# Sums of activations: their stores and loads move from SyncE's DMA queue to GpSimd's

## The chip, the cores and the metric

One core of a Trainium2 chip runs the whole program. The metric is device time in microseconds (us) of one execution; the kernel before takes 1059.25 us (median of three runs, 1059.17 to 1061.05). A core has TensorE (PE) for matmuls, VectorE (DVE), ScalarE (ACT), GpSimd (POOL) and SyncE (SP), which run side by side and wait for each other by semaphores. SP and POOL both issue DMAs here, each in the order of its own program: an instruction that waits holds up all that stand behind it on the same engine.

## The reference

```
x   = attention(q, k, v, w_phi)            # linear attention, 4 x 8 heads, 576 tokens, 64 wide
x   = (sigmoid(x @ w_gate) * (x @ w_val)) @ w_out     # 2304 tokens, 512 -> 1536 -> 512
out = leaky(x @ w_in2) @ w_out2            # 512 -> 2048 -> 512, leaky(h) = max(0.01 h, h)
```

The weights of both layers come as 64-bit floats and are decoded on the chip.

## The kernel before

**Precision.** Each operand of a matmul is kept as a high and a low part in fp32r, and a product is three matmuls (lines 52 to 54). A `gh`/`gl` pair is the two parts of a hidden activation: ACT makes `gh` (line 48), DVE makes `gl` (line 49), PE reads both.

**Stages.** Attention runs first, about 286 us, with the first units of the gated layer mixed in. Then the gated layer goes through its 1536 hidden columns in chunks of 256 (`c` = 0 to 5), and the second layer through its 2048 in eight. The tokens are five blocks: four of 512 (`b` = 0 to 3) and one of 256. Chunks 0 and 1 of the gated layer multiply block by block (`up_plain`). From chunk 2 on two blocks and two column halves are taken together by seven products instead of eight (`quad`), which needs sums and differences of the blocks of activations.

**The activation sums.** `first_sums` (line 756) makes them for one pair of blocks during chunk 1: it loads four tiles `acc` of 128x1024 from DRAM (`xd`, line 761), forms four sums on DVE (`sum_steps`, line 739), splits each into a high part on ACT (line 749) and a low part on DVE (line 750), and stores both to DRAM (`td`, line 754). Pair 0 comes first; pair 1 starts when pair 0 is done. Later, `swap` reloads them from `td` by GpSimd (line 785), or for the second layer makes them anew with `sum_parts`, stores included.

**The weights.** `decoded` (line 145) is a stream: raw 64-bit halves of 512 KB are fetched by SP into three rotating buffers (`fetch`, line 122), and six DVE and two ACT steps (lines 102 to 114) turn one into a high and a low part. A fetch waits until DVE has read the buffer that it fills. `ahead(n)` advances the stream between matmuls; `need(key)` runs it until a given piece is there; `hold` names the first piece that it may not start.

**Partial sums.** The second product of a chunk (`down1_piece`, line 666) goes from PSUM (`ps_p`, three banks) through an ACT copy (line 678) into one of six staging halves, and GpSimd adds it to DRAM with an accumulating DMA (`accd`, line 679). The next matmul group in that bank waits for the ACT copy.

**Order.** The program is written in one sequence, and a scheduling layer fixes the order of the instructions on each engine when it is built. DVE and ACT execute strictly in that order.

Of the kernel before, what the change touches and what calls it, by code (L numbers as in the profile page):

```python
# [9 lines left out]
F32 = mybir.dt.float32  # L10
# [9 lines left out]
def linear_attention_moe(ctx, tc, q, k, v, w_phi, w_gate, w_val, w_out, w_in2, w_out2, out):  # L20
    nc = tc.nc
# [43 lines left out]
    xd = [dr.tile([128, KD, MAIN], F32, name=f"xd{b}") for b in range(B)]  # L65
# [7 lines left out]
    def take(dt, name="w"):  # L73
        pool, tag = free.popleft()
        return pool.tile([128, 1024], dt, tag=tag, name=name), (pool, tag)

    def give(*slots):
        free.extend(place for _, place in slots)
# [112 lines left out]
    def drop(*key):  # L191
        r = wts.pop(key)
        give(*(r[k] for k in ("hi", "lo", "sh", "sl") if k in r))


    def hidden(h, key, src):
        w = src.shape[1]
        hi = pools["hp"].tile([128, 512], F32R, tag="gh", name="gh")[:, :w]
        lo = pools["hp"].tile([128, 512], F32R, tag="gl", name="gl")[:, :w]
        split(src, hi, lo)  # L200
        h[key] = (hi, lo)
# [274 lines left out]
    def new_pair(b, c):  # L476
        p = Pair()
        p.b, p.c = b, c
        p.kf, p.tq, p.qf, p.u = [], [], [], []
        return p  # L480
# [7 lines left out]
    n = o = oo = None  # L488
# [38 lines left out]
    for i in range(NP + 1):  # L527
        oo, o, n = o, n, (new_pair(*pairs[i]) if i < NP else None)
# [87 lines left out]
    hold = [(3, 0)]  # L616
# [11 lines left out]
    def need(*key):  # L628
        while key not in wts:
            if next(stream, None) is not True and key not in wts:  # L630
                raise RuntimeError(f"no room for {key}: {len(free)} slots free")
# [4 lines left out]
    def gap(n):  # L636
        for _ in range(n):
            if pend:
                pend.popleft()()
# [15 lines left out]
    def load_acc(b):  # L655

        for i in range(1 if b == B else 2):
            acc(1, b, 2 * i)
            a = sums[1, b, i][0]
            if b == B:  # L660
                nc.sync.dma_start(out=a.rearrange("p (k t) -> p k t", k=KD), in_=accd[b])
            else:
                nc.sync.dma_start(out=a.rearrange("p (k t) -> p k t", k=2), in_=accd[b][:, 2 * i:2 * i + 2])
# [25 lines left out]
    def up_plain(l, c, b, steps):  # L689
        w = bw[b]  # L690
        h = {}
        for f in range(CH):
            fs = slice(128 * f, 128 * f + 128)
            ps = []
            for i in range(2 if l == 1 else 1):
                need(l, c, i)
                wt = wts[l, c, i]
                p = bank("u", w)
                for kk in range(KD):
                    mm3(p, wt["vhi"][:, kk, fs], wt["vlo"][:, kk, fs], xpart(xh, b, kk), xpart(xl, b, kk), kk == 0, kk == KD - 1)  # L700
                ps.append(p)
                if l == 1 and i == 0:
                    th = tile2(w)
                    nc.scalar.activation(out=th, in_=p, func=ACTF.Tanh, scale=0.5)
            if l == 1:
                nc.vector.scalar_tensor_tensor(out=th, in0=th, scalar=1.0, in1=ps[1], op0=ALU.add, op1=ALU.mult)
                hidden(h, (f, b), th)
                if f == 0:
                    gap(4)
            else:  # L710
                leaky(h, (f, b), ps[0], True)
            ahead(steps)
        return h
# [17 lines left out]
    td = {}  # L731
    ts = {}

    def sum_steps(l, pair):

        f = {(j, i): sums[l - 1, 2 * pair + i, j][0] for j in range(2) for i in range(2)}
        b11, b12, b21, b22 = (f[j, i] for j in range(2) for i in range(2))
        for o, x, y in ((b11, b12, b11), (b12, b22, b12), (b22, b22, b11), (b21, b21, b22)):
            nc.vector.tensor_tensor(out=o, in0=x, in1=y, op=ALU.subtract)
            yield True  # L740
# [3 lines left out]
    def sum_parts(l, pair, n, s):  # L744

        j, i = PLACE[n]
        src = sums.pop((l - 1, 2 * pair + i, j))
        hi, lo = s[0][0], s[1][0]
        nc.scalar.copy(hi, src[0])
        nc.vector.tensor_tensor(out=lo, in0=src[0], in1=hi.bitcast(F32), op=ALU.subtract)  # L750
        give(src)
        td[l, pair, n] = dr.tile([128, 2, 1024], F32, name=f"td{l}{pair}{n}", tag=f"td{l}{pair}{n}")
        for k in range(2):
            nc.sync.dma_start(out=td[l, pair, n][:, k], in_=s[k][0].bitcast(F32))

    def first_sums(pair, stay):

        for i in range(2):
            for j in range(2):
                s = sums[0, 2 * pair + i, j] = take(F32, "acc")  # L760
                nc.sync.dma_start(out=s[0].rearrange("p (k t) -> p k t", k=2), in_=xd[2 * pair + i][:, 2 * j:2 * j + 2])
        for _ in range(14):
            yield True
        yield from sum_steps(1, pair)
        held = deque()
        for n in (2, 1, 3, 4):
            if len(held) == 2:
                give(*held.popleft())
            s = [take(F32R) for _ in range(2)]
            sum_parts(1, pair, n, s)  # L770
            if stay:
                ts[n] = s
            else:
                held.append(s)
            yield True
            yield True
        if not stay:
            for _ in range(4):
                yield True
        for s in held:  # L780
            give(*s)
# [9 lines left out]
    def swap(l, pair, n):  # L791

        ts[n] = [retake(s) for s in ts[n]]
        if (l, pair, n) in td:
            load_sums(l, pair, n)
        else:
            sum_parts(l, pair, n, ts[n])
# [66 lines left out]
    def up_pair1(c, pair, between, then):  # L864
        h, th = {}, {}
        for i, t in quad(1, c, 0, pair, (1, 1, 1, 1, 1, 0), lambda n: None):
            th[i] = halves[6 + i]
            nc.scalar.activation(out=th[i], in_=t, func=ACTF.Tanh, scale=0.5)
        between()
        for i, t in quad(1, c, 1, pair, (1, 1, 1, 0, 0, 0), then):  # L870
            nc.vector.scalar_tensor_tensor(out=th[i], in0=th[i], scalar=1.0, in1=t, op0=ALU.add, op1=ALU.mult)
            hidden(h, (i // 2, 2 * pair + i % 2), th[i])
        return h
# [38 lines left out]
    for b in range(B - 1, NB):  # L912
        h = up_plain(1, 0, b, 14)
# [6 lines left out]
    for b in range(NB):  # L920
# [6 lines left out]
        h = up_plain(1, 1, b, 5)  # L927
# [16 lines left out]
    for c in range(2, NC1):  # L944
        final = c == NC1 - 1
        if final:
            units = [0, 1, B]
        for n, u in enumerate(units):
            if u == B:
                h = up_plain(1, c, B, 2)  # L950
            elif not final:
                h = up_pair1(c, u, (lambda: drop(1, c, 0)) if n == 2 else (lambda: None),
                             (lambda k, u=u: swap(1, 1 - u, k)) if n == 0 else keep)
            elif u == 0:
                def between():
                    need(1, c, 1)
                    need(1, c, 2)
                    hold[0] = 2, 0

                def then(k):  # L960
                    swap(1, 1, k)
                    if k == 4:
                        gap(2)
                        load_acc(0)
                        load_acc(1)
                h = up_pair1(c, 0, between, then)
            else:
                def between():
                    gap(100)
                    drop_sums(1, c, 0)  # L970
                    side.append(sum_steps(2, 0))

                def then(k):
                    for g in side:
                        for _ in g:
                            pass
                    side.clear()
                    swap(2, 0, k)
                give(*fixed[:3])
                hold[0] = 2, 1  # L980
                h = up_pair1(c, 1, between, then)
                drop_sums(1, c, 1)
                for b in (2, 3, B):
                    load_acc(b)
                reserve[0] = 0
            gap(100)
            if n == 2:
                if final:
                    drop(1, c, 0)
                drop(1, c, 1)  # L990
            queue1(c, u, h)
            if n == 2:
                pend.append(lambda c=c: drop(1, c, 2))
        units = units[::-1]
# [7 lines left out]
    for c in range(NC2):  # L1002
        for n, u in enumerate(units):
            if u == B:
                h = up_plain(2, c, B, 1)
                gap(3)
            else:
                h = up_pair2(c, u, (lambda k, u=u: swap(2, 1 - u, k)) if n == 0 else keep)
# [41 lines left out]
```

## Time and profile before

| | |
|---|---|
| median of three runs | 1059.25 us (1059.17 to 1061.05) |
| the profiled execution | 1059.2 us; its span from first to last instruction 1057.4 us; mean granted clock 0.995 |
| PE busy | 1022.5 us, 97% of the span |
| DVE, ACT, POOL busy | 779.9, 519.6, 169.6 us |
| raw weight loads by SP | 68 of 512 KB, median 4.4 to 5.8 us from issue to landing by tensor |
| `td` stores by SP | 32 of 512 KB, median 5.0 us |
| `xd` loads by SP | 8 of 512 KB, median 8.2 us |
| `td` reloads by POOL | 88 of 512 KB, median 6.2 us |

A row of the timeline gives the start in us from the span's start, the length, engine, line, operation and what is written from what; in brackets, how long the engine stood idle before it and what ended that. A row of the windows gives for each engine the busy time and in parentheses the number of instructions, then the granted TensorE clock (1.00 is 2.4 GHz), the busy share of the DMA engines and GB/s.

### The profile page before, as it was taken

How to read it: one execution, taken by the hardware profiler on the slowest of the kernel's cores; microseconds unless marked ns; L12 is line 12 of the kernel's file. 1: busy time of each engine (PE TensorE's matmuls, PEld its weight loads, DVE VectorE, ACT ScalarE, POOL GpSimd, SP SyncE). 2: the span in 40 equal slices, each digit the busy share in tenths (PEclk: the TensorE clock that was granted, in tenths of full speed). 3: DMA queues.
4: the chain of work that ended last, by engine and by line, in shares of the span. 5: the costliest groups of instructions: out<-in, count | busy, mean ns of one | idle time of the engine just before them, and what ended most of it. 6: DMA issues, size and time to landing. Idle time of an engine off the chain costs nothing.

```text
span 1057.4 us, 15006 instructions
## 1 busy us (share of the span) xinstructions
PE 1022.5 (97%) x5410; PEld 870.3 (82%) x5410; DVE 779.9 (74%) x1373; ACT 519.6 (49%) x1066; POOL 169.6 (16%) x217
## 2 busy tenths in 40 slices
PE   7999999999999989999999989899999999999998
PEld 6788989889788778888888868788888888888886
DVE  4964877766489748395784859998797887979555
ACT  4666676767456535354454434477343333434221
POOL 0122121212201123323233120001010010101000
PEclk9999999999999999999999999999999999999999
DMA  5633343332287978769499493546161542415143
GB/s 142 162 97 93 85 111 99 82 104 75 75 304 224 349 130 256 99 153 260 66 251 187 93 303 147 209 145 221 58 233 63 183 143 97 176 63 179 42 164 134
DMA packets 119481, 160.06 MB, mean 151 GB/s; under 512 B 68720, under 2 KB 71408, under 8 KB 119408
## 3 DMA queue, kind: packets, MB, share of 16 engines
q1 hardware_dynamic: 95216, 94.09, 28.4%
q0 software_dynamic: 24192, 65.02, 24.4%
q8 instruction: 43, 0.70, 0.3%
q14 instruction: 30, 0.25, 0.1%
HBM read 109.64 MB, written 49.36 MB: 150 GB/s over the span
## 4 chain that ended last, share of the span: by engine, by line
PE 76%; issue 6%; DVE 6%; DMA 4%; ACT 3%; POOL 2%; SPq 2%; POOLq 0%; DVEq 0%; ACTq 0%
PE ps_u L53 11%; PE ps_u L52 11%; PE ps_u L54 11%; PE ps_p L52 11%; PE ps_p L54 10%; PE ps_p L53 10%; PE kv L395 4%; PE ps_n L445 2%; POOL accd L679 1%; DMA raw<-in_moe_w_gate_dram 1%; DVE ql L430 1%; POOL rb L467 1%; PE ps_q L413 1%; DMA rb<-rd 1%; DMA w<-td 1%
## 5 line engine op out<-in xcount | busy, mean ns | idle before, releaser
L824 DVE TENSOR_TENSOR q<-ps_u,q 128x512 f32<-128x512 f32 x160 | 109.8, 687 | 63.9 <-PE ps_u L54 57.7
L53 PE MATMUL ps_u<-xl,w 128*128 128x512 f32 (+1 forms) x432 | 152.0, 352 | 0.6 <-DVE xl L686 0.6
L54 PE MATMUL ps_u<-xh,w 128*128 128x512 f32 (+1 forms) x432 | 151.3, 351 | 0.0
L52 PE MATMUL ps_u<-xh,w 128*128 128x512 f32 (+1 forms) x432 | 151.3, 351 | 0.0
L894 DVE TENSOR_TENSOR acc<-acc,ps_p 128x512 f32<-128x512 f32 x126 | 86.2, 684 | 39.5 <-PE ps_p L54 39.0
L52 PE MATMUL ps_p<-w,gh 128*128 128x512 f32 x288 | 112.2, 390 | 0.0
L53 PE MATMUL ps_p<-w,gh 128*128 128x512 f32 x288 | 112.0, 389 | 0.0
L54 PE MATMUL ps_p<-w,gl 128*128 128x512 f32 x288 | 111.7, 389 | 0.0
L785 POOL DMA_DIRECT2D w<-td x88 | 48.6, 559 | 381.9 <-PE ps_u L54 366.5
L679 POOL DMA_DIRECT2D accd<-w x80 | 70.9, 891 | 229.7 <-ACT w L678 159.3
L52 PE MATMUL ps_u<-w 128*128 128x512 f32 x256 | 100.5, 393 | 1.1 <-DVE q L824 1.0
L53 PE MATMUL ps_u<-w 128*128 128x512 f32 x256 | 100.4, 392 | 0.0
L54 PE MATMUL ps_u<-w 128*128 128x512 f32 x256 | 99.9, 391 | 0.0
L53 PEld LDWEIGHTS ps_u<-xl,w 128*128 128x128 f32 x432 | 82.3, 190 | 11.8 <-DVE xl L686 0.8
L52 PEld LDWEIGHTS ps_u<-xh,w 128*128 128x128 f32 x432 | 82.0, 190 | 11.4
L54 PEld LDWEIGHTS ps_u<-xh,w 128*128 128x128 f32 x432 | 82.3, 190 | 10.8
L52 PE MATMUL ps_p<-gh,w 128*128 128x512 f32 (+1 forms) x216 | 79.0, 372 | 8.5 <-ACT gh L48 4.8
L467 POOL TENSOR_TENSOR rb<-u,rb 64x576 f32<-64x576 f32 x32 | 48.7, 1521 | 234.4 <-DMA rb<-rd 116.6
L717 ACT ACTIVATE q<-q 128x512 f32<-128x512 f32 x48 | 30.2, 632 | 112.1 <-DVE q L824 112.0
L53 PE MATMUL ps_p<-gl,w 128*128 128x512 f32 (+1 forms) x216 | 79.9, 371 | 4.1 <-DVE gl L49 3.9
L54 PE MATMUL ps_p<-gh,w 128*128 128x512 f32 (+1 forms) x216 | 79.7, 370 | 0.0
L49 DVE TENSOR_TENSOR gl<-q,gh 128x512 fp32r<-128x512 f32 (+1 forms) x102 | 61.8, 614 | 19.8 <-ACT gh L48 19.6
(151 smaller groups left out, 2304.0 us busy)
## 6 DMA issues: line engine op xcount, KB each, us to landing
w<-td POOLq DMA_DIRECT2D x88, 512.0 KB, 6.2
td<-w SPq DMA_DIRECT2D x32, 512.0 KB, 5.0
accd<-w POOLq DMA_DIRECT2D x64, 256.0 KB, 6.1
raw<-in_moe_w_out_dram SPq DMA_DIRECT2D x28, 512.0 KB, 4.5
raw<-in_moe_w_in_dram SPq DMA_DIRECT2D x16, 512.0 KB, 4.4
raw<-in_moe_w_gate_dram SPq DMA_DIRECT2D x12, 512.0 KB, 5.8
raw<-in_moe_w_val_dram SPq DMA_DIRECT2D x12, 512.0 KB, 5.0
rb<-rd SPq DMA_DIRECT2D x32, 144.0 KB, 3.1
```

Source lines behind the costliest of these rows:

```text
L49: nc.vector.tensor_tensor(out=lo, in0=src, in1=hi.bitcast(F32), op=ALU.subtract)
L52: nc.tensor.matmul(ps, lh, rh, start=first, stop=False, **kw)
L53: nc.tensor.matmul(ps, lh, rl, start=False, stop=False, **kw)
L54: nc.tensor.matmul(ps, ll, rh, start=False, stop=last, **kw)
L395: nc.tensor.matmul(ps[:, h], p.kf[j // 2][:, j % 2, h, s, :], vf[:, j, 64 * h:64 * h + 65], start=(h, j) == (0, 0), stop=False)
L445: nc.tensor.matmul(ps2, w[0], x[0], start=s == 0, stop=s == 1)
L467: nc.gpsimd.tensor_tensor(out=p.rb[sl], in0=p.u[h][sl], in1=p.rb[sl], op=ALU.mult)
L679: nc.gpsimd.dma_start(out=accd[b][:, e], in_=st, accum_op=ALU.add)
L717: nc.scalar.activation(out=th, in_=t, func=ACTF.Lrelu)
L785: nc.gpsimd.dma_start(out=ts[n][k][0].bitcast(F32), in_=td[l, pair, n][:, k])
L824: nc.vector.tensor_tensor(out=o, in0=x, in1=y, op=ALU.add)
L894: nc.vector.tensor_tensor(out=a, in0=a, in1=po, op=ALU.add)
```

## The change

The `td` stores of `sum_parts` and the `xd` loads of `first_sums` are issued by GpSimd instead of SP: 32 stores and 8 loads of 512 KB. In the last chunk of the gated layer the two `need` calls between the two products of the first pair go, and `hold` is set before the first product instead.

```diff
--- before.py
+++ after.py
@@ -751,14 +751,14 @@
         give(src)
         td[l, pair, n] = dr.tile([128, 2, 1024], F32, name=f"td{l}{pair}{n}", tag=f"td{l}{pair}{n}")
         for k in range(2):
-            nc.sync.dma_start(out=td[l, pair, n][:, k], in_=s[k][0].bitcast(F32))
+            nc.gpsimd.dma_start(out=td[l, pair, n][:, k], in_=s[k][0].bitcast(F32))
 
     def first_sums(pair, stay):
 
         for i in range(2):
             for j in range(2):
                 s = sums[0, 2 * pair + i, j] = take(F32, "acc")
-                nc.sync.dma_start(out=s[0].rearrange("p (k t) -> p k t", k=2), in_=xd[2 * pair + i][:, 2 * j:2 * j + 2])
+                nc.gpsimd.dma_start(out=s[0].rearrange("p (k t) -> p k t", k=2), in_=xd[2 * pair + i][:, 2 * j:2 * j + 2])
         for _ in range(14):
             yield True
         yield from sum_steps(1, pair)
@@ -952,10 +952,7 @@
                 h = up_pair1(c, u, (lambda: drop(1, c, 0)) if n == 2 else (lambda: None),
                              (lambda k, u=u: swap(1, 1 - u, k)) if n == 0 else keep)
             elif u == 0:
-                def between():
-                    need(1, c, 1)
-                    need(1, c, 2)
-                    hold[0] = 2, 0
+                hold[0] = 2, 0
 
                 def then(k):
                     swap(1, 1, k)
@@ -963,7 +960,7 @@
                         gap(2)
                         load_acc(0)
                         load_acc(1)
-                h = up_pair1(c, 0, between, then)
+                h = up_pair1(c, 0, lambda: None, then)
             else:
                 def between():
                     gap(100)
```

The places where order changes: the start of chunk 0's last blocks, on SP. `raw` is a fetch of weights, `accd` a partial sum, `acc<-xd` a load for the sums, `td` a store of a sum. Before:

```order
L122 DMA raw<-in_moe_w_gate_dram 128x2x512
L229 DMA accd_3624<-st 128x512
L122 DMA raw<-in_moe_w_gate_dram 128x2x512
L122 DMA raw<-in_moe_w_val_dram 128x2x512 x2
L761 DMA acc<-xd_96 128x1024 x2
L122 DMA raw<-in_moe_w_out_dram 128x1024
L761 DMA acc<-xd_97 128x1024 x2
L122 DMA raw<-in_moe_w_out_dram 128x1024
```

The four loads stood behind four fetches; they are gone from this queue. The same stretch and the next on POOL, now (`rb` is the attention's last product):

```order
L467 TENSOR_TENSOR rb<-u_3524,rb 64x576
L761 DMA acc<-xd_96 128x1024 x2
L761 DMA acc<-xd_97 128x1024 x2
L754 DMA td_4164<-w 128x1024
L754 DMA td_4171<-w 128x1024
L754 DMA td_4157<-w 128x1024
L679 DMA accd_1871<-w 128x512 x2
L754 DMA td_4157<-w 128x1024
L679 DMA accd_1871<-w 128x512
L754 DMA td_4164<-w 128x1024
L679 DMA accd_1871<-w 128x512
L754 DMA td_4171<-w 128x1024
```

They now stand first after the attention's last product, with nothing ahead of them, and the stores of pair 0 stand between the accumulating DMAs. Before, POOL had only the accumulating DMAs (L679) here. On DVE, where the sums of pair 1 begin, before:

```order
L102 TENSOR_SCALAR e_4633<-raw_4071 128x512
L111 SCALAR_TENSOR_TENSOR m_4502<-m_4502,e_4543 128x512
L109 SCALAR_TENSOR_TENSOR e_4633<-raw_4071,e_4633 128x512
L706 SCALAR_TENSOR_TENSOR q_4227<-q_4227,ps_u_4229 128x512
L49 TENSOR_TENSOR gl_4244<-q_4227,gh_4243 128x512
L739 TENSOR_TENSOR acc_4254<-acc_4258,acc_4254 128x1024
```

and now:

```order
L102 TENSOR_SCALAR e_4633<-raw_4071 128x512
L111 SCALAR_TENSOR_TENSOR m_4502<-m_4502,e_4543 128x512
L102 TENSOR_SCALAR e_4679<-raw_4541 128x512
L109 SCALAR_TENSOR_TENSOR e_4633<-raw_4071,e_4633 128x512
L706 SCALAR_TENSOR_TENSOR q_4227<-q_4227,ps_u_4229 128x512
L109 SCALAR_TENSOR_TENSOR e_4679<-raw_4541,e_4679 128x512
L49 TENSOR_TENSOR gl_4244<-q_4227,gh_4243 128x512
L739 TENSOR_TENSOR acc_4254<-acc_4258,acc_4254 128x1024
```

Two steps of decoding the next raw half (L102 and L109 of `e_4679`) moved ahead of the first sum (L739); they stood behind the fourth L750 before. Some 25 rows later a hidden activation (L706 of `q_4431`) now follows L102 of `e_4793` at once and stood behind L109 of it before. On PE the rows are the same; on DVE and ACT nothing else moved, in the last chunk of the gated layer nothing at all.

## Rows read from the trace of the kernel before

**Rows 1.** The page's first part: busy us, share, instructions.

```profile
PE 1022.5 (97%) x5410; PEld 870.3 (82%) x5410; DVE 779.9 (74%) x1373; ACT 519.6 (49%) x1066; POOL 169.6 (16%) x217
```

**Rows 2.** Waits of PE, 286 to 540 us: total us, times, longest.

```profile
PE ps_p L52 <- ACT gh L48: 4.8, 2, 3.4
PE ps_p L52 <- ACT w L678: 1.3, 1, 1.3
PE ps_p L53 <- DVE gl L49: 0.2, 1, 0.2
```

**Rows 3.** Windows behind the two longer of these waits.

```profile
304.00:308.00 4.00, 4.00 (x23) 3.34 (x22) 4.00 (x9) 2.94 (x6) 0.00 (x0) 1.00 0.92 312
...
380.00:384.00 4.00, 1.78 (x5) 1.23 (x6) 2.74 (x5) 1.59 (x4) 0.00 (x0) 0.88 0.03 8
384.00:388.00 4.00, 4.00 (x14) 3.18 (x13) 0.00 (x0) 1.01 (x3) 1.61 (x2) 0.69 0.49 59
```

**Rows 4.** Timeline of DVE from the end of attention.

```profile
294.46 0.43 DVE L102 TENSOR_SCALAR e<-raw 128x512 int32<-128x512 int32 x1 [6.95 <-issue]
...
297.72 0.43 DVE L102 TENSOR_SCALAR e<-raw 128x512 int32<-128x512 int32 x1
...
301.75 0.68 DVE L706 SCALAR_TENSOR_TENSOR q<-q,ps_u 128x512 f32<-128x512 f32 x1
```

**Rows 5.** Timeline of SP's DMA issues, same stretch.

```profile
289.26 0.39 SPq L122 DMA_DIRECT2D raw<-in_moe_w_gate_dram  x1
...
297.00 0.94 SPq L761 DMA_DIRECT2D acc<-xd  x2
```

**Rows 6.** Timeline of POOL: first issue after attention; four reloads in a burst.

```profile
332.13 1.96 POOL L679 DMA_DIRECT2D accd<-w  x2 [46.13 <-DVE acc L739]
...
408.99 2.52 POOL L785 DMA_DIRECT2D w<-td  x4 [0.30 <-PE ps_u L54]
```

**Rows 7.** Two gate fetches by line: issue, then us to landing.

```profile
L122 SPq DMA_DIRECT2D raw<-in_moe_w_gate_dram x1: 427/427/427, 291.2 to 291.2; - x1
...
DMA to landing us min/median/max: 6.5/6.5/6.5
...
L122 SPq DMA_DIRECT2D raw<-in_moe_w_gate_dram x1: 379/379/379, 409.3 to 409.3; - x1
...
DMA to landing us min/median/max: 9.6/9.6/9.6
```

**Rows 8.** Windows: accumulating DMAs start; the sums of pair 1 are loaded.

```profile
332.00:338.00 6.00, 6.00 (x28) 4.95 (x28) 6.00 (x9) 3.86 (x6) 3.61 (x4) 1.00 0.83 177
...
335.00:354.00 19.00, 19.00 (x85) 15.76 (x84) 13.78 (x23) 7.48 (x13) 3.03 (x4) 1.00 1.04 324
```

**Rows 9.** Timeline of SP: loads for pair 1, then two fetches.

```profile
340.40 5.24 SPq L761 DMA_DIRECT2D acc<-xd  x4
345.74 0.41 SPq L122 DMA_DIRECT2D raw<-in_moe_w_out_dram  x1
346.25 0.38 SPq L122 DMA_DIRECT2D raw<-in_moe_w_gate_dram  x1
```

**Rows 10.** Timeline of DVE around the sums of pair 1.

```profile
341.09 0.69 DVE L109 SCALAR_TENSOR_TENSOR e<-raw,e 128x512 int32<-128x512 int32 x1
...
352.52 2.50 DVE L739 TENSOR_TENSOR acc<-acc 128x1024 f32<-128x1024 f32 x2 [4.20 <-DMA acc<-xd]
...
366.06 0.68 DVE L706 SCALAR_TENSOR_TENSOR q<-q,ps_u 128x512 f32<-128x512 f32 x1
...
370.87 1.28 DVE L107 SCALAR_TENSOR_TENSOR m<-raw,m 128x512 f32<-128x512 uint32 x2
...
378.79 0.43 DVE L102 TENSOR_SCALAR e<-raw 128x512 int32<-128x512 int32 x1 [3.60 <-DMA raw<-in_moe_w_gate_dram]
...
380.62 0.68 DVE L706 SCALAR_TENSOR_TENSOR q<-q,ps_u 128x512 f32<-128x512 f32 x1
```

**Rows 11.** The chain that ended last, 365 to 385 us: start, us, what.

```profile
371.58 7.11 DMA raw<-in_moe_w_gate_dram
```

**Rows 12.** Waits of PE, 540 to 720 us.

```profile
PE ps_p L53 <- DVE gl L49: 3.7, 1, 3.7
```

## Prediction

> **What bounds the kernel now.** I read the busy shares first, then PE's waits by stretch, then DVE's timeline at each wait, then the DMA issues that DVE waits for. PE is busy for 97% of the span [rows 1], so the time can change by little more than PE's idle time and its time at a lower clock. The change touches DMAs between 297 and 365 us (chunk 1, where the sums are made) and between 652 and 695 us (the sums for the second layer). From 286 to 540 us PE waits four times, 6.3 us in all: 1.4 us near 303, 1.3 us near 367, and 3.4 + 0.2 us at 382 [rows 2]. The granted clock stays at 1.00 behind the wait of 1.4 us and falls to 0.88 and 0.69 in the two windows around and behind that of 3.4 us [rows 3], which is the lower level (1.2 GHz) for part of them: 4 x 0.12 + 4 x 0.31 = 1.7 us lost. The 382 us wait thus costs 5.3 us.
>
> All of them end at DVE or at ACT work that DVE feeds, and DVE is late because of transfers. At the end of attention it stands idle for 6.95 us until the first raw half is there (294.46), takes the second at 297.72, and comes in its order to the hidden activation L706 at 301.75 [rows 4], from which ACT makes the `gh` that PE waits for. At 352.52 it has waited 4.20 us for the loads of pair 1's sums [rows 10]. At 378.79 it has waited 3.60 us for a gate fetch [rows 10] that was issued at 371.58 and took 7.11 us [rows 11]; L706 at 380.62 stands behind that.
>
> **The change part by part.** The profiled execution took 1059.2 us, its span is 1057.4 us, and the median is 1059.25 us; I add to 1059.2.
>
> *The first loads of sums go earlier.* On SP they are issued from 297.00, behind four fetches [rows 5]. On POOL they stand first, and POOL issues nothing until 332.13 [rows 6]. They need what the first fetch needs, the end of attention in that memory, so they go when it goes, 289.26 [rows 5], 7.7 us earlier, four in a burst of some 2.5 us like the reloads of 408.99 [rows 6]. Nobody wants them that early: the first sum stands far behind on DVE. But the fetches at 289 and 291, for which DVE is idle, now share the DMA engines with 2 MB of sums. The second took 6.5 us without such a burst; the gate fetch at 409.3, beside the burst of reloads, took 9.6 us [rows 7]. By these the second raw half is 0 to 3.1 us later. From 294.46 on DVE is a chain without slack, in which 297.72 to 301.75 is step on step, and PE already waits at its end, so the delay goes to DVE and PE alike. The row of 409.3 is the nearest, but there up to eight loads were queued, here four: I take +2.3 us. The wait of 1.4 us becomes 3.7 us in one or two pieces; if in one, the lower clock follows as at 382 us, up to 1.7 us for PE alone. That extra lag is mostly taken back in the waits at 367 and 382 us, where PE waits for DVE anyway; what of it passes to DVE, since L706 needs PE's product, I put at +0.3 us (0 to 1.7).
>
> On how two issuing engines share, the rows above show a fetch 3.1 us slower beside POOL's burst. The Trainium skill, "DMA: Bandwidth & Descriptors" (Queues, rings and completion order; Issuing engines are not separate DMA queues), says that all queues run on the same 16 DMA engines, which take packets from them in turn, so another issuer brings no bandwidth. The row agrees; by the opposite view, separate paths, this term would be 0.
>
> *The loads for pair 1.* On SP they go out at 340.40 to 345.64, and two fetches wait behind them until 345.74 and 346.25 [rows 9]. From 335 to 354 us the DMA engines are full (share 1.04, 324 GB/s) [rows 8], so order decides and not issue. On POOL the loads cannot go earlier (they stand behind the last store of pair 0), and stores, accumulations and loads keep their order among themselves. What changes is SP: the first fetch can go when DVE has read its buffer, at 341.09 + 0.69 = 341.8 [rows 10], the second some 3 us later, and both take their share ahead of the loads. Two times 0.52 MB at 324 GB/s are 3.2 us. The sums start between 0 and 3.2 us later; I take +2.2.
>
> *DVE's order behind it.* From the first sum to the end of the first L107 are 370.87 + 0.6 - 352.52 = 19 us [rows 10], of which L102 and L109 of the moved half, 0.4 + 0.6 us, now fall into the wait ahead of the sums: -1.0. The gate fetch that follows meets no stores of SP's any more: 7.1 us [rows 11] to 6.5 us [rows 7], -0.4 (0 to -0.6). L706 then follows L102 at once, not L109 after an ACT step: 380.62 - 378.79 = 1.83 us become 0.4 to 0.5 [rows 10]: -1.3. With the sums' +2.2 the wait at 382 us ends 0.5 us earlier, set against the shift of 2.3 + 0.3. PE comes to it later by up to 1.7 us if its clock fell at 303, so the wait itself shrinks from 3.4 to about 2 us, between the 1.4 that kept the clock and the 3.4 that did not [rows 2, 3]: half a chance to save 1.7, -0.8.
>
> *Stores between accumulations.* A waiting store holds up the accumulating DMAs behind it on POOL, these the staging halves, these ACT's copy and PE's banks. The first four are issued from 332.13, and the halves are wanted again from 354 on: nothing, up to 2 us if stores land late. POOL's issues take 3.61 / 4 = 0.9 us each while DVE is busy for 6.00 of 6 us [rows 8], and 2.52 / 4 = 0.6 us in the burst [rows 6]; twelve in 11 us fit.
>
> *652 to 695 us, and the `need` calls.* The order on PE, DVE and ACT stays there, and the longest wait of PE, 3.7 us [rows 12], lies ahead of the first store. Nothing. The last-chunk edit alone moves nothing: the pieces that it no longer forces are asked for by the product that follows.
>
> Sum: +2.3 + 0.3 - 0.5 - 0.8 = +1.3; 1059.2 + 1.3 = **1060.5 us**.
>
> **Rivals.**
> 1. *The fetches keep their pace, faster.* DMA bandwidth at 289 to 297 us suffices, +0; the pair-1 fetches slip in without holding up the sums, +0. Then 1.0 + 0.4 + 1.3 = 2.7 us off at 382 us, the wait near 367 goes with an L706 two instructions earlier, and with the lower clock gone 1.7 more: 1059.2 - 2.7 to -4.4, about 1055.4. For it: the fetch at 291 still landed in 6.5 us with three others in flight. Against it: the row of 409.3.
> 2. *The full price, slower.* Decided at 289 us: if the second raw half lands over 3 us later, +3.1; the lower clock behind the longer wait passes to DVE whole, +1.7; the sums come 3.2 late, which leaves 3.2 - 1.0 - 1.3 = +0.9, and the clock still falls at 382. 1059.2 + 5.7 = 1064.9. For it: DVE has no slack from 294 to 348 us. Against it: four loads, not eight.
> 3. *POOL cannot issue beside DVE.* Longer issues would delay sums and accumulations together. The four issues of 0.9 us at a DVE that never paused [rows 8] speak against it; with the 0.3 us between 0.9 and 0.6, twelve issues cost 3.6 us, 1062.8, if all lay on the path. The Trainium skill, "SBUF — State Buffer" (SBUF: two separate sides, the trap "DVE blocks DMA"; A bandwidth-pool intuition that's wrong), says that GpSimd cannot write descriptors while DVE holds their shared port, and gives 620 ns against 3100 ns: by it twelve issues would cost 30 us, an estimate, about 1089. The row does not show it.
> 4. *The change does nothing that counts*: both collisions stay small, 1059.2.
>
> **How the numbers follow.** Less than 0.2% (2.1 us) cannot be told from no change here. My forecast, with rival 4 beside it, spans 1058 to 1062.5 and gets 0.44: 0.36 of it within 0.2%, 0.02 faster, 0.06 slower. Rival 1: 0.25, of it 0.23 faster. Rival 2: 0.27, of it 0.24 slower. Rival 3: 0.04, of it 0.03 slower. Together faster 0.25, same 0.42, slower 0.33. The range 1055.5 to 1064.5 reaches to the middle of rivals 1 and 2.
>
> **What would show it.** The four loads of `acc` on POOL near 289 to 292 us; DVE's L102 of 297.72 later by about 2.3 us and PE's wait near 303 of about 3.7 us; the first sum of pair 1 some 2 us later still; PE's wait at 382 us shorter, with the clock at 1.00 or nearly. From 400 us on PE's waits as before. I am wrong if the second raw half lands within 7 us of its issue, if the sums of pair 1 start earlier than before relative to PE, or if PE's waits after 540 us change.

## The result and the profile after

The changed kernel takes 1066.07 us (median of seven runs, 1064.81 to 1070.02); seven runs of the kernel before beside them have a median of 1061.05 us. The ratio is 1.0053, with a 95% interval of 1.0033 to 1.0073: slower by 5.6 us (the medians lie 5.0 us apart). The profiled execution took 1064.81 us, its span is 1063.0 us, 5.6 us longer than before. The prediction had 1060.5 us and a range up to 1064.5. It added to 1059.2 us, and seven runs put the kernel before 1.8 us higher, which is not the change's doing; 5.6 us added to 1059.2 are 1064.8, also outside the range.

PE's busy time grew by 1.9 us [rows 1] and its idle time by 3.7. The page's first part, changed kernel:

```profile
PE 1024.4 (96%) x5410; PEld 871.6 (82%) x5410; DVE 780.3 (73%) x1373; ACT 519.9 (49%) x1066; POOL 191.8 (18%) x257
```

PE's waits from 286 to 540 us, changed kernel (total us, times, longest): 10.7 us against 6.3 [rows 2].

```profile
PE ps_p L52 <- ACT gh L48: 5.7, 2, 3.3
PE ps_p L52 <- ACT w L678: 2.2, 1, 2.2
PE ps_p L53 <- DVE gl L49: 2.1, 2, 1.7
PE ps_u L52 <- ACT q L704: 0.7, 1, 0.7
```

Where they lie, in the timeline of PE (start, length; in brackets the wait and what ended it):

```profile
298.45 0.39 PE L52 MATMUL ps_u<-xh,w 128*128 128x256 f32 x1 [0.71 <-ACT q L704]
302.12 0.50 PE L53 MATMUL ps_p<-gl,w 128*128 128x512 f32 x1 [1.75 <-DVE gl L49]
306.45 0.73 PE L52 MATMUL ps_p<-gh,w 128*128 128x512 f32 x2 [2.42 <-ACT gh L48]
...
356.95 0.50 PE L52 MATMUL ps_p<-gh,w 128*128 128x512 f32 x1 [2.19 <-ACT w L678]
...
387.21 0.50 PE L52 MATMUL ps_p<-gh,w 128*128 128x512 f32 x1 [3.26 <-ACT gh L48]
```

Three waits stand where one of 1.4 us stood. Windows behind the third of them and behind the last; the third number from the end is the granted clock, and they answer to [rows 3]:

```profile
304.00:308.00 4.00, 1.58 (x7) 1.32 (x7) 4.00 (x9) 1.82 (x3) 0.00 (x0) 0.92 0.34 131
308.00:312.00 4.00, 4.00 (x14) 3.21 (x13) 3.69 (x8) 2.69 (x5) 0.00 (x0) 0.66 0.33 89
...
388.00:392.00 4.00, 3.97 (x12) 3.19 (x13) 0.73 (x2) 1.58 (x3) 1.05 (x2) 0.66 0.24 21
```

From 304 to 312 us the clock is at its lower level (1.2 GHz) for part of the time: 4 x 0.08 + 4 x 0.34 = 1.7 us, which were not lost there before. The cause stands in the DMA issues at the end of attention, which answer to [rows 5] and [rows 6]. POOL's, in its timeline:

```profile
289.22 2.29 POOL L761 DMA_DIRECT2D acc<-xd  x4 [3.90 <-issue]
```

and SP's, in the same stretch:

```profile
288.58 0.39 SPq L122 DMA_DIRECT2D raw<-in_moe_w_gate_dram  x1
290.18 0.32 SPq L229 DMA_DIRECT2D accd<-st  x1
290.55 0.43 SPq L122 DMA_DIRECT2D raw<-in_moe_w_gate_dram  x1
```

The timeline of DVE shows who waits for them; it answers to [rows 4] and [rows 10]:

```profile
298.43 0.69 DVE L706 SCALAR_TENSOR_TENSOR q<-q,ps_u 128x512 f32<-128x512 f32 x1 [3.43 <-ACT q L704]
...
301.04 0.43 DVE L102 TENSOR_SCALAR e<-raw 128x512 int32<-128x512 int32 x1 [1.32 <-DMA raw<-in_moe_w_gate_dram]
...
305.06 0.68 DVE L706 SCALAR_TENSOR_TENSOR q<-q,ps_u 128x512 f32<-128x512 f32 x1
...
354.13 0.43 DVE L102 TENSOR_SCALAR e<-raw 128x512 int32<-128x512 int32 x1 [3.82 <-DMA raw<-in_moe_w_out_dram]
...
359.73 2.49 DVE L739 TENSOR_TENSOR acc<-acc 128x1024 f32<-128x1024 f32 x2 [2.60 <-DMA acc<-xd]
...
385.47 0.43 DVE L102 TENSOR_SCALAR e<-raw 128x512 int32<-128x512 int32 x1 [3.77 <-DMA raw<-in_moe_w_gate_dram]
385.81 0.68 DVE L706 SCALAR_TENSOR_TENSOR q<-q,ps_u 128x512 f32<-128x512 f32 x1
```

Read from the issue of the first fetch (288.58, before 289.26 [rows 5]: attention ended 0.7 us earlier in this execution), the second raw half is taken 3.32 + 0.68 = 4.0 us later than before, and L706 as well. The fetch issued at 290.55 took 10.5 us, where 6.5 were [rows 7]:

```profile
L122 SPq DMA_DIRECT2D raw<-in_moe_w_gate_dram x1: 428/428/428, 290.6 to 290.6; - x1
...
who waited for it (us, times):
  DVE e L102: 1.3, 1
...
DMA to landing us min/median/max: 10.5/10.5/10.5
```

There is a second victim: the last partial sum of attention (L229, 256 KB), issued at 290.18. ACT's L704 needs the buffer that it empties; it landed in 7.5 us, and in 4.3 in the kernel before. Changed kernel:

```profile
L229 SPq DMA_DIRECT2D accd<-st x1: 320/320/320, 290.2 to 290.2; - x1
...
who waited for it (us, times):
  ACT q L704: 3.7, 1
...
DMA to landing us min/median/max: 7.5/7.5/7.5
```

Kernel before:

```profile
L229 SPq DMA_DIRECT2D accd<-st x1: 319/319/319, 290.9 to 290.9; - x1
...
DMA to landing us min/median/max: 4.3/4.3/4.3
```

Matching the starts of PE's matmuls one by one, the changed kernel is 0.7 us early at 280 us, 4.9 us late at 320, 5.3 at 400, 5.6 at the end. So 5.5 us are lost between 289 and 312 us: 4.0 of waiting and 1.5 at the lower clock. (The rows above give 4.9 - 1.4 = 3.5 and 1.7; the ends of matmuls in a trace are modelled, so the idle times are less sure than the starts.) Another 0.4 are lost between 320 and 400, and 0.35 behind.

### The profile page after: what moved, and what is told of

Same layout as the page of the kernel before. It is cut to its first block, busy times and chain, and to the rows that moved or that the text cites. A ratio compares the mean times of both kernels' runs of the same rounds, so it can differ in the third digit from the quotient of the medians.

```text
span 1063.0 us, 14997 instructions
## 1 busy us (share of the span) xinstructions
PE 1024.4 (96%) x5410; PEld 871.6 (82%) x5410; DVE 780.3 (73%) x1373; ACT 519.9 (49%) x1066; POOL 191.8 (18%) x257
## 4 chain that ended last, share of the span: by engine, by line
PE 76%; DVE 8%; issue 5%; DMA 5%; ACT 3%; POOL 2%; SPq 2%; POOLq 0%; ACTq 0%; DVEq 0%
PE ps_p L52 11%; PE ps_p L54 11%; PE ps_p L53 11%; PE ps_u L53 10%; PE ps_u L52 10%; PE ps_u L54 10%; PE kv L395 4%; DMA raw<-in_moe_w_gate_dram 2%; PE ps_n L445 2%; DVE ql L430 1%; DMA acc<-xd 1%; POOL accd L679 1%; PE ps_q L413 1%; DVE acc L739 1%; PE ps_t L328 1%
## 5 line engine op out<-in xcount | busy, mean ns | idle before, releaser
L679 POOL DMA_DIRECT2D accd<-w x80 | 71.3, 895 | 169.6 <-ACT w L678 132.7
L54 PEld LDWEIGHTS ps_u<-xh,w 128*128 128x128 f32 x432 | 82.3, 191 | 10.8
```

Source lines behind the costliest of these rows:

```text
L54: nc.tensor.matmul(ps, ll, rh, start=False, stop=last, **kw)
L679: nc.gpsimd.dma_start(out=accd[b][:, e], in_=st, accum_op=ALU.add)
```

## The experiments

Ratios are against runs of the kernel before on the same chip, with 95% intervals. Theory A is the collision at 289 us; theory B, that POOL's order and DVE's new order between 330 and 390 us make the loss. Of the kernels with a changed DVE order it is said; where nothing is said, PE, DVE and ACT keep the order of the kernel they start from. The `need` edit alone leaves the order of every engine as it was and was not run.

**Only the loads of pair 0 on POOL** (kernel before):

```diff
-nc.sync.dma_start(out=s[0]...
+(nc.gpsimd if pair == 0 else nc.sync).dma_start(out=s[0]...
```

> The kernel before with one thing changed: the four loads of pair 0's sums go from SP to POOL, so that they are issued at the end of attention. PE, DVE and ACT keep their order. Theory A (collision: these four loads share the DMA engines with the first raw halves and nearly all of the loss is this): the second raw half lands 10 us or more after its issue instead of 6.5, PE's waits between 297 and 307 us sum to 4.5 to 5 us, the lower clock follows; PE is about 5.5 us late at 320 us, and where PE waits for DVE at 367 and 382 us up to 1.5 of it comes back: 4 to 5.5 us slower than before, ratio 1.004 to 1.005. Theory B (the loss is made by POOL's order and DVE's new order between 330 and 390 us; a delay at 303 us would be taken back in the waits at 367 and 382 us): the lag is gone by 400 us, within 1 us of before.

1.0055 (1.0034 to 1.0077): the whole loss, by four of the forty moved DMAs. PE's waits near 300 us are those of the changed kernel (0.3, 1.65 and 2.44 us), and the second raw half took nearly as long:

```profile
DMA to landing us min/median/max: 10.0/10.0/10.0
```

Of the clock's share nothing came back later; PE's waits from 330 to 400 us:

```profile
PE ps_p L52 <- ACT gh L48: 3.8, 1, 3.8
PE ps_p L52 <- ACT w L678: 1.2, 1, 1.2
```

These are the waits of before (3.4 and 1.3 us, [rows 2]). DVE was as late as PE there, since its transfers wait for PE: the loads of pair 1 went out at 344.35 instead of 340.40 us [rows 9]. By PE's starts 5.0 us are lost near 300 us and 1.2 more at 382 to 396 us, where the wait is 0.4 us longer and the clock stays at its lower level for longer: 0.71, 0.50 and 0.94 in the windows of 4 us from 384 us on, against 0.88 and 0.69 from 380 us on before [rows 3].

**All of the change but these four loads** (changed kernel, line 761):

```diff
-nc.gpsimd.dma_start(out=s[0]...
+(nc.gpsimd if pair == 1 else nc.sync).dma_start(out=s[0]...
```

> The changed kernel with the four loads of pair 0's sums back on SP behind the fetches; all the rest of the change stays, and PE, DVE and ACT have the order of the changed kernel. Theory A: the wait near 303 us is 1.4 us again and the loss goes, 1 us faster to 1 us slower than before (ratio 0.999 to 1.001), since what is left cost only about 0.4 us in the changed kernel. Theory B: it keeps the loss, 4 to 5 us slower than before.

1.0010 (0.9993 to 1.0028). Theory A holds from both sides, B falls. The rest of the change is worth nothing that can be measured (-0.7 to 3.0 us). The wait near 303 us is 1.9 us in this run's trace, not 1.4, and the clock falls behind it; but that execution, of 1069.8 us, is the longest of twelve with a median of 1062.75.

**Two of the four loads on POOL** (kernel before, line 761):

```diff
-nc.sync.dma_start(out=s[0]...
+(nc.gpsimd if pair == 0 and i == 0 else nc.sync).dma_start(out=s[0]...
```

> The kernel before with two of the four loads of pair 0's sums on POOL (1 MB at the end of attention), the other two on SP where they were. Theory A with the bytes deciding: the second raw half lands 1.5 to 2.5 us later than before instead of 4, PE's waits near 303 us sum to about 3 to 3.5 us, and the time is 1.5 to 3.5 us longer, depending on the lower clock behind the wait. If the presence of a second issuing queue decides and not the bytes: the same loss as with four loads, 4 to 5.5 us. Theory B: no change.

1.0023 (1.0012 to 1.0035), so the loss goes with the bytes; a second issuer by itself would have cost what four loads cost. The second raw half took 7.7 us, between 6.5 and 10.0 (none and four loads):

```profile
DMA to landing us min/median/max: 7.7/7.7/7.7
```

That is less than was expected, and it was not what DVE waited for: the chain of waits runs over the partial sum instead (start, us, what).

```profile
291.66 6.92 DMA accd<-st
...
298.68 0.61 ACT q L704
...
299.31 0.69 DVE q L706
```

**The four loads on POOL, but later** (kernel before; line 761 on POOL for pair 0, with a dependency on an L109 of DVE, meant to be that of the first half; DVE and ACT have an order of their own, and a dozen small matmuls move on PE):

```diff
-nc.sync.dma_start(out=s[0]...
+x = (nc.gpsimd if pair == 0 else nc.sync).dma_start(out=s[0]...
+pair == 0 and tc.add_manual_dep(x, <an L109 of DVE>, Sync)
```

> The kernel before with the four loads of pair 0's sums on POOL, but each made to wait for DVE's L109 of the first raw half, so that POOL issues them near 296.5 us, where SP issues them in the kernel before, and not at the end of attention. (The first sum L739 and a dozen matmuls of 256 columns move by some places between 308 and 330 us.) Theory A (the collision with the first fetches and the last store of attention is the loss): the second raw half lands about 6.5 us after its issue, PE's wait near 303 us is 1.4 us again, time within 1 us of before, or 1.001 at most. Rival (a second queue with loads costs by itself, whenever it issues): 4 to 5.5 us slower, as with the early loads on POOL.

1.0007 (0.9990 to 1.0024): the second half took 6.46 us, PE's wait near 303 us is 1.45 us. But the loads did not go out near 296.5 us, as was meant. POOL waited until a later step of DVE was done:

```profile
317.25 2.29 POOL L761 DMA_DIRECT2D acc<-xd  x4 [29.83 <-DVE w L114]
```

That is 28 us behind the changed kernel's loads and 20 us behind those of the kernel before, when the fetches of 289 us have long landed; the first sum came some 17 us later, and the time is that of before. So loads on POOL do not cost by themselves, as far as a run with DVE's order changed can say: the rival falls. That they cost nothing at 296.5 us, or as much from SP at 289 us, no run shows.

**Only the stores on POOL** (changed kernel, line 761; DVE and ACT have an order of their own):

```diff
-nc.gpsimd.dma_start(out=s[0]...
+nc.sync.dma_start(out=s[0]...
```

> The changed kernel with all eight loads for the sums back on SP; only the td stores are on POOL (DVE and ACT have an order of their own around the sums of pair 1). Theory A: no early loads, so no loss near 303 us; stores alone are worth 0 to 2 us gained between 340 and 390 us, since SP's loads and fetches of pair 1 no longer stand behind stores. Theory B: stores between accumulating DMAs hold POOL up, 2 us or more slower than before.

1.0041 (1.0027 to 1.0054): my expectation was wrong, and B's reason is not what the trace shows. The new order puts the first L739 of pair 1 ahead of a `gl` that PE needs, and it waits there for its load:

```profile
345.67 1.22 DVE L739 TENSOR_TENSOR acc<-acc 128x1024 f32<-128x1024 f32 x1 [6.03 <-DMA acc<-xd]
346.81 0.68 DVE L49 TENSOR_TENSOR gl<-q,gh 128x512 fp32r<-128x512 f32 x1
```

PE waits 2.36 us for that `gl`. As the order changed with the queue, this run says nothing of the stores by themselves.

**Pair 1's stores behind the gate fetch of 371 us** (kernel before; the eight stores are held back in the program and queued on SP behind that fetch):

```diff
-nc.sync.dma_start(out=td[l, pair, n][:, k], ...)
+late.append(...)                  # pair 1 of the gated layer
+with tc.issue_after(the fetch): nc.sync.dma_start(...)
```

> The kernel before with the eight td stores of pair 1 queued on SP behind the gate fetch for which DVE waits at 378.79 us; PE, DVE and ACT keep their order. Theory A (a fetch that DVE needs is late because DMAs that nobody waits for are ahead of it on the same DMA engines): with 4 MB less in flight the gate fetch issued near 371 us lands in 4 to 5.5 us instead of 7.1, DVE's wait of 3.6 us falls to 1 to 2 us, PE's wait at 382 us to between 1 and 2 us, and where it stays under some 1.5 us the granted clock behind it stays at 1.00: 1.5 to 4 us faster than before. Rival (that fetch is slow because of its own issue or of the accumulating DMAs beside it, not because of the stores): within 0.5 us of before, or slower, if the val fetch behind the stores comes late.

1.0019 (1.0001 to 1.0037), a miss. The fetch took 8.6 us instead of 7.1 [rows 11]; being first in the queue did not protect it.

**The same stores held until 383 us** (kernel before; a dependency on ACT's L48 in place of the position in the queue):

```diff
-with tc.issue_after(the fetch): nc.sync.dma_start(...)
+x = nc.sync.dma_start(...)
+tc.add_manual_dep(x, <L48 near 383 us>, Sync)
```

> The kernel before with the eight td stores of pair 1 held back on SP until ACT's L48 near 383 us, when the gate fetch that was issued near 371 us has long landed; PE, DVE and ACT keep their order. (Where the stores stood right behind that fetch it landed in 8.6 us instead of 7.1, with 4 MB sharing the DMA engines.) Theory A (any large transfer in flight beside a needed fetch slows it, whichever stands first in the queue): the gate fetch lands in 4 to 5.5 us, DVE's wait of 3.6 us falls to 0.5 to 2 us, PE's wait of 3.4 us at 382 to 0.3 to 2 us, with less of the lower clock behind it: 1.5 to 4.5 us faster than before, ratio 0.996 to 0.9985. Rival (the fetch is slow by the accumulating DMAs beside it, which are still there): it lands in 7 us as before, within 0.5 us of before.

1.0069 (1.0048 to 1.0090), the wrong way. With no store near it the fetch still took 8.5 us:

```profile
DMA to landing us min/median/max: 8.5/8.5/8.5
```

The stores now met the next fetch, which took 10.5 us:

```profile
407.44 0.43 DVE L102 TENSOR_SCALAR e<-raw 128x512 int32<-128x512 int32 x1 [4.10 <-DMA raw<-in_moe_w_val_dram]
```

The later fetch repeats the lesson of 289 us. The slow first one is what the rival said, and the window shows what was left beside the fetch (DMA share and GB/s are the last two):

```profile
372.00:378.00 6.00, 6.00 (x35) 5.26 (x34) 3.83 (x7) 1.21 (x2) 1.88 (x3) 1.00 1.02 129
```

The DMA engines are full while they move 129 GB/s; in [rows 8] they were full at 324. In that window the accumulating DMAs (L679) and two fetches are under way.

**The changed kernel with both repairs**, the edits of the second kernel above and of the last one:

```diff
-nc.gpsimd.dma_start(out=s[0]...
+(nc.gpsimd if pair == 1 else nc.sync).dma_start(out=s[0]...
+tc.add_manual_dep(<store of pair 1, on SP>, <L48 near 383 us>, Sync)
```

> The changed kernel with two things altered: the loads of pair 0's sums back on SP behind the fetches, and the stores of pair 1 on SP but held back until near 383 us; the stores of pair 0, the loads of pair 1 and all stores of the second layer stay on POOL. PE, DVE and ACT have the order of the changed kernel. Theory A: no loss near 303 us, and the gate fetch near 378 us lands in 4 to 5.5 us, so that PE's wait at 386 us shrinks; 1 to 4 us faster than before and 6 to 9 us faster than the changed kernel. Rival (DVE's new order, with a fetch waited for ahead of L706 near 354 us, costs 2 us on its own): no better than before, 0 to 1 us slower.

1.0054 (1.0031 to 1.0078): the held stores cost here as well, DVE waits 4.25 us at 407.95 us for the same fetch.

**Chunk 1's partial sums without accumulation** (kernel before; this leaves chunk 0's part out of the sums):

```diff
-nc.gpsimd.dma_start(out=accd[b][:, e], in_=st, accum_op=ALU.add)
+nc.gpsimd.dma_start(out=accd[b][:, e], in_=st, **({} if c == 1 else {"accum_op": ALU.add}))
```

> The kernel before with the partial sums of chunk 1 stored plainly instead of accumulated (so that chunk 0's part is left out of the sums); the order of every engine stays. When the stores of pair 1 were moved away, the gate fetch issued near 371 us still took 8.5 us; the accumulating DMAs were what was left beside it. If they slow it: it lands in 4 to 5.5 us, PE's wait at 382 us falls under 2 us and the kernel is 1 to 5 us faster. If not: 7 us or more again, within 1 us of before.

0.9933 (0.9917 to 0.9949). The fetch, issued at 369.27 us, with plain sums beside it; the last store of pair 1 had landed at 367.5:

```profile
DMA to landing us min/median/max: 5.1/5.1/5.1
```

The wait at 382 us falls to 0.6 us, that near 367 is gone, and the sums of pair 1 wait 1.3 us instead of 4.2 [rows 10]. With the stores held until 383 us the fetch had no store beside it either, and took 8.5 us. So accumulation is what slows that stretch; whether by the reading of the sums in DRAM or otherwise stays open.

**Four raw buffers** (kernel before; one buffer less in pool `q`, which by itself changes no order; DVE and ACT have an order of their own):

```diff
-raws = deque(fetch(keys[n // 2], n % 2, 3) for n in range(3))
+raws = deque(fetch(keys[n // 2], n % 2, 4) for n in range(4))
-ahead = 2 * n + i + 3
+ahead = 2 * n + i + 4
```

> The kernel before with four rotating raw buffers instead of three (a fetch goes out one half earlier; one of six buffers of the pool q goes to make room, which alone leaves the order of every engine as it was). DVE and ACT get an order of their own here. Theory A (time is lost where a raw half that DVE needs lands late, and a fetch issued earlier has the slack that it lacks): the fetch now issued near 371 us goes out with the one of 346 us and has landed when DVE comes to it, DVE's wait of 3.6 us and PE's of 3.4 us at 382 go, with the lower clock behind: 3 to 5 us faster than before. At 289 us four fetches instead of three leave together, so the wait near 303 us may grow by 0 to 2 us. Rival (each earlier fetch slows those it now shares the DMA engines with, and the loss moves there): within 1 us of before, or slower.

0.9969 (0.9953 to 0.9984), faster than both kernels. PE's waits from 286 to 540 us are 4.9 us instead of 6.3, and none of them is 3.4 us long:

```profile
PE ps_p L52 <- ACT gh L48: 2.9, 2, 1.8
PE ps_p L52 <- ACT w L678: 1.8, 1, 1.8
PE ps_p L53 <- DVE gl L49: 0.2, 1, 0.2
```

**The changed kernel with four raw buffers** (the edit of the kernel just shown; DVE and ACT have an order of their own), and **the same with pair 0's loads on SP**:

```diff
-nc.gpsimd.dma_start(out=s[0]...
+(nc.gpsimd if pair == 1 else nc.sync).dma_start(out=s[0]...
```

> The changed kernel with four rotating raw buffers. Theory A: the collision at 289 us stays or grows, as four fetches and four loads of sums leave together: the second raw half lands 10 us or more after its issue and 5 us or more are lost by 310 us; the later waits shrink as in the kernel before with four buffers, so it stays 4 to 7 us slower than that one. Rival (with a buffer more the early loads no longer cost): equal to it.

> The changed kernel with four raw buffers and the loads of pair 0's sums back on SP; the order of PE, DVE and ACT is that of the changed kernel with four buffers. Theory A (the early loads are all that costs): 3 to 4 us faster than the changed kernel with four buffers, 3 to 5 us faster than before, the same as or up to 1 us faster than the kernel before with four buffers. Rival (POOL's queue of stores, accumulations and loads costs by itself where fetches have slack): it stays at the time of the changed kernel with four buffers, within 1 us of before.

1.0003 (0.9992 to 1.0015) and 0.9963 (0.9949 to 0.9976). With slack in the fetches the early loads still cost some 4 us (1.0003 - 0.9963), no more than the lower end of what was expected; the second half took 10.8 us with them. In the trace of the kernel with the early loads PE's waits near 300 us are those of the changed kernel (1.4, 1.4 and 2.45 us), but the clock stays at 1.00 from 304 to 312 us: its 1.7 us do not follow from these waits every time. The rest of the change costs nothing here either: 0.9963 and 0.9969 cannot be told apart, and both are faster than the kernel before.

## Why the prediction was wrong

The step that failed is "The first loads of sums go earlier". Its mechanism was right, and rival 2 had its outcome (1064.9); both its sizes were too small.

- *The second raw half, "0 to 3.1 us later", I took 2.3.* It was 4.0 (10.5 - 6.5). The row of the fetch beside the burst of reloads [rows 7] was no upper bound: there the fetch stood alone in front of eight loads, here a partial sum and two more fetches left with four loads in the same 2.5 us, and the DMA engines were full (share 0.94 and 1.03 from 292 to 300 us). The last two loads had also stood behind a fifth fetch on SP, at 301.29 us, so they moved 11 us, not 7.7. Two loads made the half 1.2 us later, four 4.0 or 3.5.
- *A transfer that I did not list.* The partial sum of 290.18 us was slowed from 4.3 to 7.5 us and held up DVE's L706 of 298.43 us and PE first. The prediction put this at nothing without a reason. With two loads it alone set the chain.
- *The lower clock, "mostly taken back", I took +0.3.* The clock cost 1.5 to 1.7 us and stayed. I had counted on PE's waits at 367 and 382 us as slack that DVE makes; DVE is itself fed by PE, and the waits were as long as before when only pair 0's loads had moved.

Together 5.5 us were lost where 2.6 were forecast. The Trainium skill, "DMA: Bandwidth & Descriptors" (Issuing engines are not separate DMA queues), says that another issuer saves only issue time, since all transfers interleave on the same 16 engines. The runs agree: on POOL at 289 us four loads cost 5.8 us and two 2.4, on POOL at 317 us four cost nothing that can be measured.

The terms between 340 and 400 us, -1.3 in all, came to +0.4:

- *Sums of pair 1, +2.2.* They began 7.2 us later (359.73 against 352.52), 2.3 more than PE's lag of 4.9: right in size. The two fetches did slip ahead, at 346.66 and 349.40 us, with the DMA engines full as before (share 1.04 from 340 to 359 us). But the loads also went out later, at 347.60 and 349.66 us, behind the stores on POOL; from the first issue to the third landing it is 12.0 us in both kernels. Which of the two made the 2.3 us was not separated, so the size may be luck.
- *L102 and L109 ahead of the sums, -1.0.* Wrong: the moved L102 waits 3.82 us for its own raw half, with an L706 behind it; on ACT the copies L678 stand behind the L48 that waits for this L706, so PE waits 2.2 us near 357 us, where it did not wait before. It takes the place of the wait of 1.3 us at 367 us.
- *The gate fetch, -0.4.* It took 7.3 us, not 6.5: SP's stores were gone from the queue, but the last of POOL's was still in flight beside it (issued at 374.24 us, landed in 6.5), and the accumulating DMAs slow it without any store, as the held stores showed.
- *L706 at once behind L102, -1.3.* Right: 0.34 us instead of 1.83.
- *Half a chance to keep the clock, -0.8.* The wait at 387.21 us is 3.26 us, as long as before, and the clock behind it 0.66.

"652 to 695 us" and the `need` calls at nothing were right: PE's waits there are those of before, and the 0.35 us behind 600 us are no more than where SP had kept these stores (0.15 us with only pair 0's loads moved, 2.4 with the stores behind the fetch of 371 us). Rival 3 is excluded: the four loads of pair 1 took POOL 0.53 us each to issue beside a busy DVE, and all forty moved DMAs added 191.8 - 169.6 = 22.2 us to POOL's busy time, 0.55 each. Rival 1's argument, that the fetch of 291 us had kept its pace with three others in flight, does not carry over to four more.

## What to carry to other kernels

A load that nobody waits for yet is not free: ask which transfers of the next ten microseconds are awaited, the small stores that free a buffer among them, and start it behind them; another issuing engine did not give it a lane of its own here. A lag counts as recoverable only where the waiting engine doesn't feed the one that it waits for. If fetches are late, buy slack (a fourth buffer: 0.3% here) before moving the rest out of their way: that went wrong three times here.

## What the hardware showed that was not expected

Accumulating DMAs fill the DMA engines at a low rate: 129 GB/s at a share of 1.02, with two fetches among them. Without accumulation in chunk 1 the share in the six microseconds around the same two fetches was 0.80 at 269 GB/s:

```profile
369.00:375.00 6.00, 6.00 (x35) 5.22 (x34) 3.50 (x7) 1.26 (x3) 0.54 (x1) 1.00 0.80 269
```

The first fetch took 5.1 us instead of 8.5 (7.1 in the kernel before), and POOL issued a sum in 0.54 us instead of 0.87.

What is open: how much of the fetch's 10.5 us each of its companions makes, what the stores on POOL cost or give with DVE's order held fixed, and whether the same loads from SP at 289 us would cost as much. The last two were not tried.
